# Gate and value products between the two row halves of the output products, three steps in front

## The chip, the core and the metric

The kernel runs on one core of one Trainium2 chip. The engines of the core are named as in the profile: PE (TensorE, matrix products), PEld (its weight loads), DVE (VectorE), ACT (ScalarE), POOL (GpSimd) and SP (SyncE, which here issues the transfers). The metric is the device time of one execution in microseconds (us), the median of the runs shown. A lower time is better.

## The reference

```python
scores = scale * np.matmul(x, state.transpose(0, 1, 3, 2))   # attention of x on the state, and back
...
x = np.ascontiguousarray(attn_out.transpose(0, 2, 1, 3)).reshape(B * S, H * D)   # 4352 rows x 512
x = _moe_ref(x=x, **moe_kwargs)          # soft mixture of 8 experts through 32 slots
...
g = x @ w_gate                           # 512 x 1536
silu = g * (1.0 / (1.0 + np.exp(-g)))
val = x @ w_val
return (silu * val @ w_out).astype(np.float32)
```

The last three lines are the part that the change touches. The rows of x are mixtures of 32 slots there, so the kernel multiplies the mixing weights (`cstack`) with folded gate and value weights (512 of x are folded to the slots once) instead of x with the full ones.

## The kernel before

**The main loop.** All rows are cut into 17 blocks of 256 rows (two tiles of 128), and the 1536 hidden columns into 6 pairs `q` of 2 x 128. One *step* is one block with one pair; there are 102. A function `plan()` puts the steps in order: first all blocks with pair 0, later longer runs of pairs (*segments*), so that the weights of a pair can be prepared while earlier pairs are used. The constants LEAD and RATE in it set when a new pair may come in. There are 51 segments.

A step has three parts, each a function, and their instructions go to the engines in program order; every engine works through its own queue in that order.

- `front(k)`: four products of 256 columns on PE (L1168), gates into one PSUM bank and values into another (`gvp`, two pairs of banks, taken in turn); then ACT's Silu (L1169) and DVE's product of value, scale and Silu (L1173), which writes `sh` (two buffers in turn).
- `middle(k)`: ACT's cast of that product to f16 (L1181) and POOL's difference to it (L1182): `hl`, a high and a low half.
- `back(k)`: twelve products of 512 columns on PE (L1204), six for each of the two row tiles i of the block, with `hl` as the stationary side and the output weights `WO` as the moving one. For each tile the first four products read the high half, the next two the low one. The two results stand in two of three accumulator banks `acc`, which are taken in turn: a segment's second bank is the one after the first. At a segment's last step both are evicted to `osb`, by ACT (L1231) in a block's first segment, and by DVE with an addition (L1233) in later ones.

In iteration k of the loop the order is `middle(k + 1)`, `front(k + 2)`, `back(k)`, the evictions of k, and then `spend`, which issues a bit of the background work. `hl` has two buffers, so the cast of k + 1 writes what `back(k - 1)` read.

**The background work** prepares the weights of the next pairs: POOL and DVE turn 64 bit words into f32 (`to32`: POOL L723, ACT L725, DVE L732 and L736), PE folds gates and values (L847), PE, DVE and ACT find their scales (L779 to L897), and ACT and DVE split the output weights (L812, L816). It is a generator with credits; each iteration takes 2 credits of it, or 1 where DVE has evictions to do. A fold comes one iteration or more after its last conversion was issued.

PSUM has eight banks: four for gates and values, three accumulators, one for the small products.

Of the kernel before, what the change touches and what calls it, by code (L numbers as in the profile page):

```python
# [8 lines left out]
F16 = mybir.dt.float16  # L9
# [3 lines left out]
AF = mybir.ActivationFunctionType  # L13
# [29 lines left out]
LEAD, RATE = 6, 21  # L43
# [41 lines left out]
def attn_moe_glu_kernel(  # L85
# [884 lines left out]
    def prep_first():  # L970
# [13 lines left out]
        for k in range(4):  # L984
            p2s.append((psum(k, [128, 512]) if k < 2 else gvp[1][k - 2])[:, 0:128])
            r = slice(32 * k, 32 * k + 32)
            pe.matmul(out=p2s[k], lhsT=Jrep[r, :], rhs=gt[r, :], start=True, stop=True)
# [67 lines left out]
    with tc.manual_schedule():  # L1055
# [90 lines left out]
        gvp = [[psum(3 + 2 * i + v, [128, 512]) for v in range(2)] for i in range(2)]  # L1146
# [8 lines left out]
        hls = [hlt[:, i] for i in range(2)]  # L1155

        def front(k, part=3):
            if k >= len(steps):
                return
            seg, bi, t0, q, _, _ = steps[k]  # L1160
            p, sh = gvp[k % 2], shs[k % 2]
            if part & 1:
                while 2 * q + 1 not in GV:
                    next(bg, None)
                rhs = cstack[:, t0:t0 + 2, :].rearrange("p t s -> p (t s)")
                for v in range(2):
                    for i in range(2):
                        pe.matmul(out=p[v][:, 256 * i:256 * i + 256], lhsT=GV[2 * q + i][v], rhs=rhs, start=True, stop=True)  # L1168
                act.activation(out=sh[:, 0, :], in_=p[0], func=AF.Silu, scale=sgs[q])  # L1169
            if part & 2:  # L1170
                while 2 * seg[1] - 1 not in GV:
                    next(bg, None)
                dve.scalar_tensor_tensor(out=sh[:, 1, :], in0=p[1], scalar=(kap0[0] if k == 0 else seg_scale(*seg)[0][q]), in1=sh[:, 0, :],  # L1173
                                         op0=ALU.mult, op1=ALU.mult)

        def middle(k):
# [3 lines left out]
            t = hls[k % 2]  # L1180
# [6 lines left out]
        def back(k):  # L1187
# [6 lines left out]
            accs = [acc[(2 * nblk[0] + i) % 3] for i in range(2)]  # L1194
            order = [(i, j, u) for i in range(2) for us in ((0, 1), (2,)) for j in range(2) for u in us]
            if k == 0:
                order.sort(key=lambda x: (x[1:] == (1, 1), x[2], x[1]))
            for i, j, u in order:
                while 2 * q + j not in WO:
                    next(bg, None)  # L1200
                c = slice(256 * j + 128 * i, 256 * j + 128 * i + 128)
                if i and k == len(steps) - 1:
                    continue
                pe.matmul(out=accs[i], lhsT=t[:, u // 2, c], rhs=WO[2 * q + j][:, u % 2, :],  # L1204
                          start=first and u == 0 and j == 0, stop=last and (j, u) == order[-1][1:])
            if k == len(steps) - 1:
                assert first
                for h in range(2):
                    hs = slice(256 * h, 256 * h + 256)
                    ph = (accs[1], psmall([128, 512]))[h]  # L1210
                    for n, (_, j, u) in enumerate(order[6:]):
                        c = slice(256 * j + 128, 256 * j + 256)
                        pe.matmul(out=ph[:, hs], lhsT=t[:, u // 2, c], rhs=WO[2 * q + j][:, u % 2, hs],  # L1213
                                  start=n == 0, stop=n == 5)
                    ends.append(ph)
            for i in range(2):
                a = accs[i]
                if not last:
                    continue
                o = osb[bi // 2][:, 2 * (bi % 2) + i, :]  # L1220
                rsc = segk[d, a_][1]
                if k == len(steps) - 1 and i:
                    r0 = ((t0 - 2) // 4) * ROWS + ((t0 - 2) % 4) * 128 + 128 * i
                    for h in range(2):
                        hs = slice(256 * h, 256 * h + 256)
                        dve.scalar_tensor_tensor(out=o[:, hs], in0=ends[h][:, hs], scalar=rsc, in1=o[:, hs],  # L1226
                                                 op0=ALU.mult, op1=ALU.add)
                        nc.sync.dma_start(out=out[r0:r0 + 128, hs], in_=o[:, hs])
                    continue
                if d == 0:  # L1230
                    act.activation(out=o, in_=a, func=AF.Copy, scale=rsc)  # L1231
                else:
                    dve.scalar_tensor_tensor(out=o, in0=a, scalar=rsc, in1=o, op0=ALU.mult, op1=ALU.add)  # L1233
                if k == len(steps) - 1:
                    r0 = ((t0 - 2) // 4) * ROWS + ((t0 - 2) % 4) * 128 + 128 * i
                    nc.sync.dma_start(out=out[r0:r0 + 128, :], in_=o)
# [10 lines left out]
            if t0:  # L1247
                r0 = ((t0 - 2) // 4) * ROWS + ((t0 - 2) % 4) * 128
# [21 lines left out]
        front(1, 2)  # L1270
        for k in range(len(steps)):
            middle(k + 1)
            front(k + 2)
            back(k)
            seg = steps[min(k + 4, len(steps) - 1)][0]
# [64 lines left out]
```

## Time and profile before

| | us |
|---|---|
| median of three runs | 470.25 (469.53 to 470.87) |
| the profiled execution | 469.4 |
| its span, first to last instruction | 467.6 |
| PE busy | 443.3 |
| DVE, ACT, POOL busy | 299.5, 251.1, 178.1 |
| span of the main loop's products, first L1204 start to its last | 138.4 to 462.5 |

A product that follows another is listed with its whole pass, so that rows overlap; the busy share of PE is therefore no measure of how many columns it took in. What matters is where PE stood idle, and what ended that.

### The profile page before, as it was taken

To read this page: it belongs to the slowest core of one execution; us is meant where nothing else is said; L and a number is where in the kernel's file an instruction comes from. 1 tells how busy PE (TensorE), PEld (TensorE's weight loads), DVE (VectorE), ACT (ScalarE), POOL (GpSimd) and SP (SyncE) were. 2 spreads that over 40 slices of the span, in tenths; PEclk is the share of its full clock that TensorE was granted. 3 is DMA by queue.
4 is the path that set the end of the run, shared out by engine and by line. 5 is a ranking of instruction groups with operands and counts; after the bars stand their busy time and mean duration, and the time that the engine had idled before them with its cause. 6 is when DMAs were issued, how large, how long until landed. Compare 5 with 4: busy or idle time off the path is not lost. (4 is left out here: it accounts for less than half of the span.)

```text
span 467.6 us, 9564 instructions
## 1 busy us (share of the span) xinstructions
PE 443.3 (95%) x3723; PEld 245.4 (52%) x3723; DVE 299.5 (64%) x629; ACT 251.1 (54%) x439; POOL 178.1 (38%) x160
## 2 busy tenths in 40 slices
PE   8799998999989999998998999999999999999997
PEld 6576765544454545444454454555555555555553
DVE  3777988467657888888998975544333433434555
ACT  2587877427348998764563535444444444444441
POOL 0113122073018656553573743433333333333331
PEclk9899999999999999999999999999999999999999
DMA  8999999799999407000000000000011111121224
GB/s 313 423 421 411 416 418 410 296 368 423 403 420 420 166 9 273 10 4 6 7 1 7 6 3 12 1 0 2 0 46 45 46 46 47 45 90 46 90 89 182
DMA packets 20060, 75.04 MB, mean 160 GB/s; under 512 B 5424, under 2 KB 7088, under 8 KB 13104
## 3 DMA queue, kind: packets, MB, share of 16 engines
q1 hardware_dynamic: 20016, 74.45, 40.1%
q8 instruction: 29, 0.48, 0.4%
q14 instruction: 15, 0.12, 0.1%
HBM read 64.87 MB, written 8.91 MB: 158 GB/s over the span
## 5 line engine op out<-in xcount | busy, mean ns | idle before, releaser
L1204 PE MATMUL p<-wo,hl 128*128 128x512 f16 x1014 | 233.9, 379 | 5.9 <-DVE osb L1233 3.0
L1182 POOL TENSOR_TENSOR hl<-sh,hl 128x512 f16<-128x512 f32 x102 | 123.4, 1210 | 198.3 <-PE p L1168 108.8
L1204 PEld LDWEIGHTS <-hl 128*128 128x128 f16 x1218 | 118.3, 98 | 131.3 <-POOL hl L1182 6.0
L1173 DVE SCALAR_TENSOR_TENSOR sh<-p,segk,sh 128x512 f32<-128x512 f32 x102 | 76.3, 748 | 102.5 <-ACT sh L1169 98.6
L1181 ACT CAST hl<-sh 128x512 f16<-128x512 f32 x102 | 62.9, 616 | 118.4 <-PE p L1204 90.4
L1169 ACT ACTIVATE sh<-p,sg 128x512 f32<-128x512 f32 x85 | 58.2, 685 | 5.6 <-PE p L1168 0.6
L1233 DVE SCALAR_TENSOR_TENSOR osb<-p,segm,osb 128x512 f32<-128x512 f32 x67 | 48.9, 745 | 11.6 <-PE p L1204 11.6
L1204 PE MATMUL p<-bqm,hl 128*128 128x512 f16 x204 | 47.0, 379 | 0.0
L1168 PE MATMUL p<-cstack,gvs 128*128 128x256 f16 x272 | 41.1, 273 | 0.6 <-DVE sh L1173 0.6
L357 POOL TENSOR_TENSOR a<-a,r 128x1024 f32<-128x1024 f32 x7 | 13.4, 1914 | 57.3 <-DVE r L353 16.3
L1168 PEld LDWEIGHTS <-gvs 128*128 128x128 f16 x272 | 25.8, 98 | 16.5 <-issue 1.8
L732 DVE SCALAR_TENSOR_TENSOR u<-u 128x512 uint32<-128x512 uint32 (+1 forms) x33 | 24.5, 753 | 5.1 <-POOL u L723 5.0
L723 POOL TENSOR_SCALAR u<-u 128x512 uint32<-128x512 uint8 x30 | 26.8, 892 | 2.5
L736 DVE SCALAR_TENSOR_TENSOR gvf<-gvf,u 128x512 uint32<-128x512 uint32 (+1 forms) x22 | 21.5, 994 | 0.2
L1168 PE MATMUL p<-cstack,gv 128*128 128x256 f16 x136 | 20.4, 273 | 0.0
L315 PE MATMUL p<-cs,atA 128*128 128x128 f32 x128 | 18.5, 285 | 1.7 <-DVE atA L280 0.5
L1231 ACT ACTIVATE osb<-p,segk 128x512 f32<-128x512 f32 x28 | 18.4, 693 | 2.7 <-PE p L1204 2.6
L310 ACT ACTIVATE atA<-atA,nm 128x512 f32<-128x512 f32 x16 | 10.7, 719 | 13.6 <-PE p L315 13.6
L1168 PEld LDWEIGHTS <-gv 128*128 128x128 f16 x136 | 13.2, 98 | 8.5
L315 PEld LDWEIGHTS p<-cs,atA 128*128 128x128 f32 x128 | 15.0, 146 | 3.6 <-DVE atA L280 1.0
L676 PE MATMUL p<-u,exq 128*32 128x256 f32 x256 | 15.2, 381 | 1.6 <-DMA u<-in_w_dram 0.8
L725 ACT ACTIVATE gvf<-u 128x512 f32<-128x512 f32 (+1 forms) x22 | 14.9, 723 | 0.0
(217 smaller groups left out, 452.9 us busy)
## 6 DMA issues: line engine op xcount, KB each, us to landing
u<-in_w_dram SPq DMA_DIRECT2D x24, 1024.0 KB, 14.5
u<-in_wgv_dram SPq DMA_DIRECT2D x12, 1024.0 KB, 17.4
u<-in_xn_dram SPq DMA_DIRECT2D x8, 1040.0 KB, 18.0
out_dram<-osb SPq DMA_DIRECT2D x15, 512.0 KB, 2.8
early<-in_w_dram SPq DMA_DIRECT2D x12, 512.0 KB, 10.4
u<-in_wo_dram SPq DMA_DIRECT2D x6, 1024.0 KB, 17.2
u<-in_xt_dram SPq DMA_DIRECT2D x3, 1024.0 KB, 7.1
early<-in_w_dram SPq DMA_DIRECT2D x1, 1024.0 KB, 8.9
```

Source lines behind the costliest of these rows:

```text
L315: pe.transpose(p[:, j, q * 128:(q + 1) * 128], stsA[:, q, j * 128:(j + 1) * 128], ident)
L723: pool.tensor_scalar(out=lo[:, c], in0=byte[:, c], scalar1=2.0 ** -5, scalar2=-31.0 / 64, op0=ALU.mult, op1=ALU.add)
L732: dve.scalar_tensor_tensor(out=lo[:, c], in0=hi[:, c], scalar=0x80000000, in1=lo[:, c], op0=ALU.bitwise_and, op1=ALU.bitwise_or)
L736: dve.scalar_tensor_tensor(out=tu[:, c], in0=tu[:, c], scalar=3, in1=lo[:, c], op0=ALU.logical_shift_left, op1=ALU.bitwise_or)
L1168: pe.matmul(out=p[v][:, 256 * i:256 * i + 256], lhsT=GV[2 * q + i][v], rhs=rhs, start=True, stop=True)
L1169: act.activation(out=sh[:, 0, :], in_=p[0], func=AF.Silu, scale=sgs[q])
L1173: dve.scalar_tensor_tensor(out=sh[:, 1, :], in0=p[1], scalar=(kap0[0] if k == 0 else seg_scale(*seg)[0][q]), in1=sh[:, 0, :], op0=ALU.mult ...
L1181: act.copy(out=t[:, 0, :], in_=sh[:, 1, :])
L1182: pool.tensor_tensor(out=t[:, 1, :], in0=sh[:, 1, :], in1=t[:, 0, :], op=ALU.subtract)
L1204: pe.matmul(out=accs[i], lhsT=t[:, u // 2, c], rhs=WO[2 * q + j][:, u % 2, :], start=first and u == 0 and j == 0, stop=last and (j, u) == ...
L1231: act.activation(out=o, in_=a, func=AF.Copy, scale=rsc)
L1233: dve.scalar_tensor_tensor(out=o, in0=a, scalar=rsc, in1=o, op0=ALU.mult, op1=ALU.add)
```

## The change

The iteration becomes: first half of `back(k)` (tile 0) and its eviction, `front(k + 3)`, `middle(k + 2)`, second half of `back(k)` (tile 1) and its eviction, background work. `back` is now a generator that is left and entered again between its halves (not at step 0, where all twelve products come first). The buffers of `hl` become three; the third lies where an early tile of the kernel (`sp`) had been. Before the loop, `middle(1)` and `front(2)` are issued as well. The bank pairs and the three accumulators are the same banks as before, written in another form. LEAD goes from 6 to 7, which moves the joints between segments from step 24 on (there are 51 segments as before), and `seg_scale` looks one step further ahead.

```diff
@@ -40,7 +40,7 @@
 H2 = 0
 H7 = 0
 HP_ = 0, 1
-LEAD, RATE = 6, 21
+LEAD, RATE = 7, 21
 CR = 1.0
 CN = 2.0
 YM = 5
@@ -982,7 +982,7 @@
         gv = [gvs[:, 0, v] for v in range(2)]
         p2s = []
         for k in range(4):
-            p2s.append((psum(k, [128, 512]) if k < 2 else gvp[1][k - 2])[:, 0:128])
+            p2s.append((psum(k, [128, 512]) if k < 2 else gvp[k])[:, 0:128])
             r = slice(32 * k, 32 * k + 32)
             pe.matmul(out=p2s[k], lhsT=Jrep[r, :], rhs=gt[r, :], start=True, stop=True)
         mw = sm.tile([128, 1], F32, tag="mw1", bufs=1, name="mw")
@@ -1143,7 +1143,7 @@
         expert_o(1)
         ps1.close()
         ps.append(ctx.enter_context(tc.tile_pool(name="ps2", bufs=1, space=PSUM)))
-        gvp = [[psum(3 + 2 * i + v, [128, 512]) for v in range(2)] for i in range(2)]
+        gvp = [psum(3 + i, [128, 512]) for i in range(4)]
         steps = []
         for bi, d, a in plan():
             for q in range(d, a):
@@ -1152,13 +1152,13 @@
         osb = {}
         shs = [wk.tile([128, 2, 512], F32, tag=f"a{i}", name="sh") for i in range(2)]
         hlt = wk.tile([128, 2, 2, 512], F16, tag="e2", name="hl")
-        hls = [hlt[:, i] for i in range(2)]
+        hls = [hlt[:, i] for i in range(2)] + [wk.tile([128, 2, 512], F16, tag="sp", name="hl")]
 
         def front(k, part=3):
             if k >= len(steps):
                 return
             seg, bi, t0, q, _, _ = steps[k]
-            p, sh = gvp[k % 2], shs[k % 2]
+            p, sh = [gvp[(2 * k + v) % 4] for v in range(2)], shs[k % 2]
             if part & 1:
                 while 2 * q + 1 not in GV:
                     next(bg, None)
@@ -1177,7 +1177,7 @@
             if k >= len(steps):
                 return
             sh = shs[k % 2]
-            t = hls[k % 2]
+            t = hls[k % 3]
             act.copy(out=t[:, 0, :], in_=sh[:, 1, :])
             pool.tensor_tensor(out=t[:, 1, :], in0=sh[:, 1, :], in1=t[:, 0, :], op=ALU.subtract)
             hl[k] = t
@@ -1192,48 +1192,48 @@
                 room[0] -= 1
                 room[1] -= 1
             accs = [acc[(2 * nblk[0] + i) % 3] for i in range(2)]
+            end = k == len(steps) - 1
             order = [(i, j, u) for i in range(2) for us in ((0, 1), (2,)) for j in range(2) for u in us]
             if k == 0:
                 order.sort(key=lambda x: (x[1:] == (1, 1), x[2], x[1]))
-            for i, j, u in order:
-                while 2 * q + j not in WO:
-                    next(bg, None)
-                c = slice(256 * j + 128 * i, 256 * j + 128 * i + 128)
-                if i and k == len(steps) - 1:
-                    continue
-                pe.matmul(out=accs[i], lhsT=t[:, u // 2, c], rhs=WO[2 * q + j][:, u % 2, :],
-                          start=first and u == 0 and j == 0, stop=last and (j, u) == order[-1][1:])
-            if k == len(steps) - 1:
-                assert first
-                for h in range(2):
-                    hs = slice(256 * h, 256 * h + 256)
-                    ph = (accs[1], psmall([128, 512]))[h]
-                    for n, (_, j, u) in enumerate(order[6:]):
-                        c = slice(256 * j + 128, 256 * j + 256)
-                        pe.matmul(out=ph[:, hs], lhsT=t[:, u // 2, c], rhs=WO[2 * q + j][:, u % 2, hs],
-                                  start=n == 0, stop=n == 5)
-                    ends.append(ph)
-            for i in range(2):
-                a = accs[i]
-                if not last:
-                    continue
-                o = osb[bi // 2][:, 2 * (bi % 2) + i, :]
-                rsc = segk[d, a_][1]
-                if k == len(steps) - 1 and i:
-                    r0 = ((t0 - 2) // 4) * ROWS + ((t0 - 2) % 4) * 128 + 128 * i
+            parts = [order, []] if k == 0 else [order[0:6], order[6:12]]
+            r0 = ((t0 - 2) // 4) * ROWS + ((t0 - 2) % 4) * 128
+            for part in range(2):
+                i = part
+                if end and i:
+                    assert first and last
                     for h in range(2):
                         hs = slice(256 * h, 256 * h + 256)
-                        dve.scalar_tensor_tensor(out=o[:, hs], in0=ends[h][:, hs], scalar=rsc, in1=o[:, hs],
-                                                 op0=ALU.mult, op1=ALU.add)
-                        nc.sync.dma_start(out=out[r0:r0 + 128, hs], in_=o[:, hs])
-                    continue
-                if d == 0:
-                    act.activation(out=o, in_=a, func=AF.Copy, scale=rsc)
+                        ph = (accs[1], psmall([128, 512]))[h]
+                        for n, (_, j, u) in enumerate(parts[1]):
+                            c = slice(256 * j + 128, 256 * j + 256)
+                            pe.matmul(out=ph[:, hs], lhsT=t[:, u // 2, c], rhs=WO[2 * q + j][:, u % 2, hs],
+                                      start=n == 0, stop=n == 5)
+                        ends.append(ph)
                 else:
-                    dve.scalar_tensor_tensor(out=o, in0=a, scalar=rsc, in1=o, op0=ALU.mult, op1=ALU.add)
-                if k == len(steps) - 1:
-                    r0 = ((t0 - 2) // 4) * ROWS + ((t0 - 2) % 4) * 128 + 128 * i
-                    nc.sync.dma_start(out=out[r0:r0 + 128, :], in_=o)
+                    for x, j, u in parts[part]:
+                        while 2 * q + j not in WO:
+                            next(bg, None)
+                        c = slice(256 * j + 128 * x, 256 * j + 128 * x + 128)
+                        pe.matmul(out=accs[x], lhsT=t[:, u // 2, c], rhs=WO[2 * q + j][:, u % 2, :],
+                                  start=first and u == 0 and j == 0, stop=last and (j, u) == order[-1][1:])
+                if last:
+                    o = osb[bi // 2][:, 2 * (bi % 2) + i, :]
+                    rsc = segk[d, a_][1]
+                    if end and i:
+                        for h in range(2):
+                            hs = slice(256 * h, 256 * h + 256)
+                            dve.scalar_tensor_tensor(out=o[:, hs], in0=ends[h][:, hs], scalar=rsc, in1=o[:, hs],
+                                                     op0=ALU.mult, op1=ALU.add)
+                            nc.sync.dma_start(out=out[r0 + 128:r0 + 256, hs], in_=o[:, hs])
+                    elif d == 0:
+                        act.activation(out=o, in_=accs[i], func=AF.Copy, scale=rsc)
+                    else:
+                        dve.scalar_tensor_tensor(out=o, in0=accs[i], scalar=rsc, in1=o, op0=ALU.mult, op1=ALU.add)
+                    if end and not i:
+                        nc.sync.dma_start(out=out[r0:r0 + 128, :], in_=o)
+                if not part:
+                    yield
             if k == len(steps) - 1:
                 assert t0
                 return
@@ -1245,7 +1245,6 @@
             ob = osb[bi // 2]
             c = 2 * (bi % 2)
             if t0:
-                r0 = ((t0 - 2) // 4) * ROWS + ((t0 - 2) % 4) * 128
                 nc.sync.dma_start(out=out[r0:r0 + 256, :].rearrange("(i p) d -> p i d", p=128), in_=ob[:, c:c + 2, :])
             else:
                 for b in range(B):
@@ -1268,11 +1267,15 @@
         acc = [psum(i, [128, 512]) for i in range(3)]
         middle(0)
         front(1, 2)
+        middle(1)
+        front(2)
         for k in range(len(steps)):
-            middle(k + 1)
-            front(k + 2)
-            back(k)
-            seg = steps[min(k + 4, len(steps) - 1)][0]
+            half = back(k)
+            next(half)
+            front(k + 3)
+            middle(k + 2)
+            run(half)
+            seg = steps[min(k + 5, len(steps) - 1)][0]
             if k and all(2 * q + 1 in GV for q in range(*seg)):
                 seg_scale(*seg)
             spend(bg, CR if steps[k][5] and steps[k][0][0] else CN)
```

Three places show how instructions move on an engine. POOL, at the start of the main loop (`hl` is written by L1182 of `middle`, `u` by L723, the first part of a conversion; the L622 rows belong to the stage before the loop):

```order
 L622 TENSOR_TENSOR cc_1658<-cc,cc_1658 128x2x32 x2
-L1182 TENSOR_TENSOR hl<-sh,hl 128x512 x2
+L1182 TENSOR_TENSOR hl<-sh,hl 128x512 x3
 L723 TENSOR_SCALAR u<-u 128x512 x2
 L1182 TENSOR_TENSOR hl<-sh,hl 128x512
```

The first conversion stood behind the low halves of steps 0 and 1, and stands behind those of 0, 1 and 2 now.

ACT, in iterations 21 to 23 before (`two_2864` is the scaled fold of pair 3, which needs DVE's scales; `hl` the cast, `sh` the Silu, `wo16` the output weights):

```order
L1181 CAST hl_1978<-sh_1976 128x512
L1169 ACTIVATE sh_1977<-p5_1974,sg_2335 128x512
L890 ACTIVATE two_2864<-bqm_1980,sc_2856 128x128
L1181 CAST hl_1978<-sh_1977 128x512
L1169 ACTIVATE sh_1976<-p3_1972,sg_2335 128x512
L1181 CAST hl_1978<-sh_1976 128x512
L1169 ACTIVATE sh_1977<-p5_1974,sg_2601 128x512
L812 ACTIVATE wo16_2930<-wof_2728,sc_2856 128x512 x2
```

and the same place after the change:

```order
L1169 ACTIVATE sh_1976<-p3_1972,sg_2344 128x512
L1181 CAST hl_1979<-sh_1977 128x512
L890 ACTIVATE two_2873<-bqm_1981,sc_2865 128x128
L1169 ACTIVATE sh_1977<-p5_1974,sg_2344 128x512
L1181 CAST hl_1978<-sh_1976 128x512
L1169 ACTIVATE sh_1976<-p3_1972,sg_2610 128x512
L1181 CAST hl_1978<-sh_1977 128x512
L812 ACTIVATE wo16_2939<-wof_2737,sc_2865 128x512 x2
```

The cast that stood right behind L890 was that of step 23, which PE takes in the next iteration; it is that of step 24 now, and step 23's cast stands ahead of L890. Within an iteration the Silu comes before the cast.

DVE, where the weights of pair 4 are split (L816), before (`osb` by L1233 are the two evictions of one block; `sh` is L1173):

```order
L897 SCALAR_TENSOR_TENSOR two_3174<-bqm_1980,sc_3167,two_3174 128x128
L816 SCALAR_TENSOR_TENSOR wo16_3222<-wof_3048,sc_3167,wo16_3222 128x512 x2
L1173 SCALAR_TENSOR_TENSOR sh_1977<-p6_1975,segk_2816,sh_1977 128x512
L1233 SCALAR_TENSOR_TENSOR osb_2373<-p2_2066,segm_2815,osb_2373 128x512
L1233 SCALAR_TENSOR_TENSOR osb_2373<-p0_2064,segm_2815,osb_2373 128x512
L736 SCALAR_TENSOR_TENSOR gvf_3105<-gvf_3105,u_2419 128x512
```

and after (the eviction has the line number 1232 there):

```order
L897 SCALAR_TENSOR_TENSOR two_3187<-bqm_1981,sc_3180,two_3187 128x128
L1232 SCALAR_TENSOR_TENSOR osb_2374<-p2_2067,segm_2824,osb_2374 128x512
L1173 SCALAR_TENSOR_TENSOR sh_1977<-p6_1975,segk_3142,sh_1977 128x512
L1232 SCALAR_TENSOR_TENSOR osb_2374<-p0_2065,segm_2824,osb_2374 128x512
L816 SCALAR_TENSOR_TENSOR wo16_3231<-wof_3057,sc_3180,wo16_3231 128x512 x2
L1173 SCALAR_TENSOR_TENSOR sh_1976<-p4_1973,segk_3142,sh_1976 128x512
```

The first eviction of a block stands ahead of the product L1173 of the iteration and the second behind it, and here both stand ahead of the split that was ahead of them.

## Rows read from the trace of the kernel before

**Rows 1.** The page's costliest groups: busy us, mean ns of one | idle before.

```profile
L1204 PE MATMUL p<-wo,hl 128*128 128x512 f16 x1014 | 233.9, 379 | 5.9 <-DVE osb L1233 3.0
```

**Rows 2.** PE's waits over the whole program: in total us, times, longest.

```profile
PE p L1204 <- DVE osb L1233: 3.0, 4, 1.5
PE p L1204 <- POOL hl L1182: 1.9, 5, 0.9
...
PE p L1204 <- ACT hl L1181: 1.0, 2, 0.8
...
PE s L847 <- DVE gvf L736: 0.9, 2, 0.4
...
PE s L785 <- DVE D L783: 0.3, 1, 0.3
```

**Rows 3.** Timeline of one undisturbed step: start us, us, engine, line; idle before.

```profile
301.21 0.62 ACT L1181 CAST hl<-sh 128x512 f16<-128x512 f32 x1 [1.63 <-PE p L1204]
...
301.45 0.60 PE L1168 MATMUL p<-cstack,gv 128*128 128x256 f16 x4
...
301.88 2.75 PE L1204 MATMUL p<-wo,hl 128*128 128x512 f16 x12
301.91 1.15 POOL L1182 TENSOR_TENSOR hl<-sh,hl 128x512 f16<-128x512 f32 x1 [1.87 <-PE p L1168]
301.93 0.69 ACT L1169 ACTIVATE sh<-p,sg 128x512 f32<-128x512 f32 x1
302.70 0.75 DVE L1173 SCALAR_TENSOR_TENSOR sh<-p,segk,sh 128x512 f32<-128x512 f32 x1 [2.27 <-ACT sh L1169]
...
304.91 2.75 PE L1204 MATMUL p<-bqm,hl 128*128 128x512 f16 x12
```

**Rows 4.** Timeline, iterations 0 to 4, with the first fold.

```profile
140.84 1.92 POOL L723 TENSOR_SCALAR u<-u 128x512 uint32<-128x512 uint8 x2
141.02 1.26 ACT L1231 ACTIVATE osb<-p,segk 128x512 f32<-128x512 f32 x2 [0.90 <-PE p L1204]
...
141.47 2.75 PE L1204 MATMUL p<-wo,hl 128*128 128x512 f16 x12
...
145.27 2.41 POOL L723 TENSOR_SCALAR u<-u 128x512 uint32<-128x512 uint8 x2
...
148.99 2.57 DVE L736 SCALAR_TENSOR_TENSOR gvf<-gvf,u 128x512 uint32<-128x512 uint32 x2
...
149.48 1.90 PE L1204 MATMUL p<-wo,hl 128*128 128x512 f16 x8 [0.94 <-POOL hl L1182]
...
151.31 1.08 PE L847 MATMUL s<-gvf,ST 128*32 128x128 f32 x32
...
152.77 2.75 PE L1204 MATMUL p<-wo,hl 128*128 128x512 f16 x12
```

**Rows 5.** Timeline, iterations 22 and 23.

```profile
217.28 0.40 ACT L890 ACTIVATE two<-bqm,sc 128x128 f16<-128x128 f32 x1 [5.09 <-DVE sc L888]
217.59 0.60 ACT L1181 CAST hl<-sh 128x512 f16<-128x512 f32 x1
...
218.25 1.04 PE L1204 MATMUL p<-wo,hl 128*128 128x512 f16 x4 [0.75 <-ACT hl L1181]
```

**Rows 6.** Timeline, iterations 34 to 36.

```profile
255.61 0.74 DVE L1173 SCALAR_TENSOR_TENSOR sh<-p,segk,sh 128x512 f32<-128x512 f32 x1
256.27 1.39 DVE L1233 SCALAR_TENSOR_TENSOR osb<-p,segm,osb 128x512 f32<-128x512 f32 x2
...
257.06 1.46 PE L1204 MATMUL p<-wo,hl 128*128 128x512 f16 x6 [1.47 <-DVE osb L1233]
...
264.28 1.46 PE L1204 MATMUL p<-wo,hl 128*128 128x512 f16 x6 [1.00 <-DVE osb L1233]
```

**Rows 7.** Lines L736 and L1182 on their own: duration ns min/median/max.

```profile
L736 DVE SCALAR_TENSOR_TENSOR gvf<-gvf,u x22: 671/684/1668, 107.8 to 264.8; 128x512 uint32<-128x512 uint32 x20, 128x1024 uint32<-128x1024 uint32 x2
L1182 POOL TENSOR_TENSOR hl<-sh,hl x102: 1152/1157/3000, 138.5 to 459.3; 128x512 f16<-128x512 f32 x102
```

## The prediction

> **What bounds the kernel now.** I read the page first, then PE's waits, then the timeline of one step, then the timeline at each place where PE waits. The page's costliest group is the output product L1204 [rows 1]. In an undisturbed step, twelve of them are listed with 2.75 us, and the next twelve start 3.03 us after the first [rows 3]. With 0.379 us listed for one [rows 1], the pitch is (2.75 - 0.379) / 11 = 0.216 us; four products of the front take the remaining 3.03 - 12 x 0.216 = 0.44. So PE is full there: nothing but its own columns bounds a step, and the change takes none of them away. The 102 steps are 309 us.
>
> What it can win is the idle time in the loop, and the reader is to see in PE's waits how little that is [rows 2]: L1204 waits 3.0 us for accumulators (DVE L1233), 1.9 for the low half (POOL), 1.0 for the high half (ACT), and there are 0.9 for folds and 0.3 for a scale. A wait in this view begins when the listed 0.379 ends, not when the next product could have started, so each is 0.379 - 0.216 = 0.16 longer. With that: accumulators 3.0 + 4 x 0.16 = 3.6; POOL 1.9 + 5 x 0.16 = 2.7; ACT's large one 0.75 + 0.16 = 0.9 [rows 5]; the scale 0.4; folds 1.2. ACT's other one comes at step 0, where the change alters nothing.
>
> **The change, part by part.**
>
> *The order in ACT's and POOL's queues.* Background work of iteration k stands directly ahead of the cast and the difference for step k + 2 before, and ahead of those for k + 3 after; PE asks for those 3.03 us later. On ACT a Silu (0.69) has come between, so the delay that is borne grows by 2.3 us there and by 3.0 on POOL. The waits of this kind are 0.9 [rows 5] and at most 1.1 (0.94 + 0.16) [rows 4]. The casts themselves are no earlier: before, the difference ends 301.91 + 1.15 - 301.88 = 1.2 us after the step's start, and PE reads it at its next step's fifth product, 3.03 + 0.86; spare 2.7. After, the front begins at 6 x 0.216 = 1.3, Silu 0.48 later (301.93 - 301.45), cast and difference behind it end at about 4.2, and are read at 6.06 + 0.86; spare 2.7 again. The third `hl` buffer takes away the cast's wait for PE, 1.63 us [rows 3], which cost PE nothing. I take both sums as gone: 2.7 + 0.9 = **3.6** (bounds: 1.5, if POOL's small waits come back elsewhere, and 3.6). With the queue relieved the scale's 0.4 goes as well (bounds 0 and 0.4).
>
> *The accumulators.* Before, the evictions of a block stand behind L1173 on DVE, which is late: L1173 at 255.61, then both evictions, then PE [rows 6]. After, the first stands ahead of it: 0.66 us (256.27 - 255.61). Its bank is asked for again six products, a front and six products later before (12 x 0.216 = 2.6, and 0.44), and with another front after: 0.44 more. Together 1.1 us of each wait; the two large ones are 1.47 + 0.16 and 1.00 + 0.16 [rows 6]. The second bank is asked for as long after the first as before. LEAD moves the evictions of this stretch to other steps, and the split L816 now stands behind them. I take all **3.6** (bounds: 2.2 from the 1.1 twice, and 3.6).
>
> *Folds: the cost.* DVE's background work of iteration k stands behind L1173 of step k + 3, not k + 2. Where ACT evicts, nothing else stands ahead of it: it starts at 1.3 + 1.25 + 0.75 = 3.3 us of the step after, and at 302.70 + 0.75 - 301.88 = 1.6 before; 1.7 later. The fold on PE is only one front (0.44) later, so 1.3 us of spare are lost at each of the first three folds. Later, where DVE evicts, the work is behind the second eviction both times and nothing is lost in the order itself.
>
> The first fold is the worst place, since POOL's queue there begins late. Before, POOL's first conversion starts at 140.84 [rows 4]. After, it is behind the difference of step 2, which is behind ACT's first eviction (141.02), Silu and cast (about 0.6 each, 142.8) and its own 1.16: 144.0. The second conversion was at 145.27, and its L736 ended at 148.99 + 2.57 = 151.56, which is 6.3 later. After, it is behind the difference of step 3, whose cast comes after an eviction, two L725, an eviction and a Silu on ACT (about 0.6 each: 146.1), so that the difference ends at about 147.4 to 148.0; plus 6.3 is 153.7 to 154.3. The second half of the fold (0.5) needs it, and the step behind starts at 154.4 to 155.0 against 152.77 before. PE without a wait would reach the fold at 141.47 + 3 x 3.03 = 150.6 and that step at 151.7, so the wait is about **3.0** us where there was none; the wait of 1.1 ahead of it, counted as gone above, is given back, and more. Bounds: 1.8, if the two L736 take 0.68 each and not 2.57 together, and 4.0, if one more of DVE's two-input passes meets POOL (1.67 against 0.68) [rows 7]. Second and third fold: 1.3 for both together beyond what they wait for now (bounds 0 and 2.6; the middle, as part of ACT's lateness there goes too). Fourth and fifth: 0.5 (bounds 0 and 2), since DVE is behind there and loses its pauses.
>
> What the durations hang on here is that L736 takes from 0.67 to 1.67 us and the difference from 1.15 to 3.0 [rows 7]; the long ones lie beside each other. The Trainium skill, "SBUF — State Buffer", "Who interferes with whom", says why: a VectorE instruction with two SBUF inputs and a GpSimd one that reads SBUF exclude each other, and the one that comes second stands still until the first has ended. The trace agrees. By that rule a change that moves POOL's differences onto DVE's conversions would lose up to 1.16 us at each meeting; the 4.0 above would become 4.2.
>
> *Edits at nothing.* The halves cost PE no switch, as there are as many changes between front and back as before (the next product starts 0.43 us after a front's first, 301.88 - 301.45). `middle(1)` and `front(2)` ahead of the loop are issued in the same order on each engine. The third buffer lies where nothing is in use. At the end the last step's first eviction is the only thing that moves, and PE's last products set the end.
>
> **The sum.** 3.6 + 0.4 + 3.6 = 7.6 won, 3.0 + 1.3 + 0.5 = 4.8 lost: 2.8 us. On the profiled execution's own 469.4 this gives 466.6. That execution is 0.85 below the median of the runs shown, 470.25, from which it gives 467.45. I say **467.0**, between both.
>
> **Rivals.**
>
> *Nothing left over.* DVE is behind from iteration 20 to 36, and PE's waits are only how the delay shows. Then the accumulators keep 3.6 - 2.2 = 1.4, fourth and fifth fold cost 2, and 7.6 - 1.4 - (3.0 + 1.3 + 2) = -0.1 is left: 469.5 to 470.35. For it: DVE's row at 256.27 follows L1173 without a pause. Against: the first eviction is 1.1 us better off.
>
> *Slower: the folds.* Every fold waits as the first does, because conversion and fold are still an iteration apart while the conversion's engines run behind later steps. Five times 3.0 less the 1.2 of now is 13.8 lost, 6.2 more than won: 475.6 to 476.5. It turns slower (by more than 0.3%, or 1.4 us, which is about what a measurement of this kernel can tell from no change) once the folds wait (7.6 + 1.2 + 1.4) / 5 = 2.0 us on average. For it: the first one, worked out above, and the two L736 of 2.57 us. Against: the later ones have no start in which POOL's queue is shifted by a whole step, and for the last two the order on DVE is no worse.
>
> *All won.* The first fold waits only 1.8 and the others no longer than now: 7.6 - 1.8 = 5.8, so 463.6 to 464.5. For it: at the first fold PE's wait lets all other engines get ahead, so that later ones meet finished work.
>
> **Chances.** Forecast 0.47 (465 to 468.6), nothing left 0.25, folds 0.12, all won 0.16. The range from 463.4 to 470.9 leaves out most of the slow rival and little else. Faster by over 0.3% (under 468.8): the forecast nearly whole and all won, 0.62. Within 0.3%: 0.25. Slower: 0.13.
>
> **What the profile after would show.** PE's waits for `hl` from ACT and POOL behind step 0 gone, and the one for L1233 at or near nothing. Instead a wait of L847 for L736, of 2 to 4 us, near 151, with the step behind it at about 154.7. The step at 3.03 us in the second half of the loop, and ACT's cast there following the Silu without a wait for PE. The prediction is wrong if the step is longer than 3.03, if PE waits for a gate bank (L1168 for L1173), or if the folds after the first wait over 1.5 us each.

## The result, and the profile after

| | before | after |
|---|---|---|
| median us (6 runs each) | 469.51 (468.11 to 470.87) | 474.80 (473.54 to 478.39) |
| profiled execution, its span | 469.4, 467.6 | 473.88, 472.1 |
| first to last start of the output products in the loop | 138.4 to 462.5 | 139.0 to 467.0 |

The changed kernel is slower: 1.012 of the time before, 95% interval 1.0079 to 1.0161. The span grew by 4.5 us: 0.6 ahead of the loop (its start lies between 136.8 and 139.6 in the kernels measured here, none of which changes anything there) and 3.9 in it.

PE's waits in the loop of the changed kernel (140 to 462 us; in total us, times, longest) answer to [rows 2]:

```profile
PE s L847 <- DVE gvf L736: 6.8, 4, 2.5
PE s L785 <- DVE D L783: 1.8, 1, 1.8
PE p L1218 <- DVE osb L1232: 1.2, 1, 1.2
```

All waits for `hl` are gone, and the accumulators' are down from four to one. But the folds (L847) went from 0.9 to 6.8 and a scale (L785) from 0.3 to 1.8. With the prediction's 0.16 added to each, PE's idle time in the loop is 9.8 + 6 x 0.16 = 10.8 now. Before it was 6.9 + 13 x 0.16 = 9.0 (in the same stretch; ACT's first wait of [rows 2] lies ahead of it). That is 1.8 of the 3.9.

The rest is the clock. The page's row of granted clock, 40 slices of 11.8 us, falls in the second slice, long before the loop, and once more within it:

```profile
PEclk9799999999999999998999999999999999999999
```

The windows around that place (us; then busy time and instructions of PE, PEld, DVE, ACT, POOL; granted clock, DMA share, GB/s):

```profile
139.00:221.50 82.50, 73.82 (x459) 37.85 (x460) 67.64 (x128) 62.00 (x109) 51.54 (x44) 1.00 0.35 138
221.50:225.00 3.50, 3.50 (x12) 1.55 (x11) 3.36 (x12) 0.36 (x2) 0.00 (x0) 0.51 0.01 2
225.00:460.00 235.00, 233.76 (x1288) 121.18 (x1287) 129.50 (x227) 102.11 (x174) 99.15 (x86) 1.00 0.09 32
```

For 3.5 us PE runs at 0.51, the lower of its two levels (1.2 GHz), and does half the work: 1.7 us lost. The row before it in the timeline is the long wait for the scale, which ends at 220.89. So 1.8 + 1.7 = 3.5 of the 3.9 are accounted for. Before, the loop had no such slice.

The timeline shows the three folds that wait, and the scale (after; [rows 4] are the first fold before):

```profile
144.69 1.91 POOL L723 TENSOR_SCALAR u<-u 128x512 uint32<-128x512 uint8 x2
...
148.42 2.25 POOL L723 TENSOR_SCALAR u<-u 128x512 uint32<-128x512 uint8 x2
...
150.07 2.71 DVE L732 SCALAR_TENSOR_TENSOR u<-u 128x512 uint32<-128x512 uint32 x2
...
151.22 0.41 PE L847 MATMUL s<-gvf,ST 128*32 128x128 f32 x4
...
152.71 0.74 DVE L1173 SCALAR_TENSOR_TENSOR sh<-p,segk,sh 128x512 f32<-128x512 f32 x1
153.37 1.28 DVE L736 SCALAR_TENSOR_TENSOR gvf<-gvf,u 128x512 uint32<-128x512 uint32 x2
...
154.10 1.23 PE L847 MATMUL s<-gvf,ST 128*32 128x128 f32 x28 [2.47 <-DVE gvf L736]
...
155.26 1.04 PE L1218 MATMUL p<-wo,hl 128*128 128x512 f16 x4
...
172.66 2.75 PE L1218 MATMUL p<-wo,hl 128*128 128x512 f16 x12
...
173.56 2.59 DVE L816 SCALAR_TENSOR_TENSOR wo<-wof,sc,wo 128x512 f16<-128x512 f32 x2
...
176.07 0.68 DVE L732 SCALAR_TENSOR_TENSOR u<-u 128x512 uint32<-128x512 uint32 x1
...
177.08 0.41 PE L847 MATMUL s<-gvf,ST 128*32 128x128 f32 x4
...
178.44 1.28 DVE L736 SCALAR_TENSOR_TENSOR gvf<-gvf,u 128x512 uint32<-128x512 uint32 x2
...
179.17 1.23 PE L847 MATMUL s<-gvf,ST 128*32 128x128 f32 x28 [1.67 <-DVE gvf L736]
...
205.05 0.64 PE L847 MATMUL s<-gvf,ST 128*32 128x128 f32 x16 [2.24 <-DVE gvf L736]
...
206.11 0.63 PE L847 MATMUL s<-gvf,ST 128*32 128x128 f32 x12 [0.42 <-DVE gvf L736]
...
215.87 1.46 PE L1218 MATMUL p<-wo,hl 128*128 128x512 f16 x6
...
217.51 0.74 DVE L1173 SCALAR_TENSOR_TENSOR sh<-p,segk,sh 128x512 f32<-128x512 f32 x1
...
220.62 0.22 DVE L783 TENSOR_SCALAR D<-cs,D 3x3 f32<-3x3 f32 x1
...
220.89 0.38 PE L785 MATMUL s<-D,cs 3*128 3x3 f32 x2 [1.79 <-DVE D L783]
```

PE's first four fold products (151.22) need only the first of the fold's two converted tiles, which is long finished; the next 28 wait until DVE (L736) has written the second tile, and DVE has stood behind L1173 of a later step. The second fold shows where DVE's chain hangs, and before is the measure:

```profile
168.43 2.75 PE L1204 MATMUL p<-wo,hl 128*128 128x512 f16 x12
...
169.24 1.84 DVE L816 SCALAR_TENSOR_TENSOR wo<-wof,sc,wo 128x512 f16<-128x512 f32 x2
...
172.76 1.90 PE L1204 MATMUL p<-wo,hl 128*128 128x512 f16 x8 [0.28 <-POOL hl L1182]
...
173.25 2.26 DVE L736 SCALAR_TENSOR_TENSOR gvf<-gvf,u 128x512 uint32<-128x512 uint32 x2
...
174.59 1.60 PE L847 MATMUL s<-gvf,ST 128*32 128x128 f32 x32
...
210.12 0.75 DVE L1173 SCALAR_TENSOR_TENSOR sh<-p,segk,sh 128x512 f32<-128x512 f32 x1 [1.08 <-ACT sh L1169]
...
210.54 2.75 PE L1204 MATMUL p<-wo,hl 128*128 128x512 f16 x12
...
213.27 0.22 DVE L783 TENSOR_SCALAR D<-cs,D 3x3 f32<-3x3 f32 x1
...
213.54 0.38 PE L785 MATMUL s<-D,cs 3*128 3x3 f32 x2 [0.25 <-DVE D L783]
```

From the start of L816 to the end of the second L736 it is 173.25 + 2.26 - 169.24 = 6.3 us before, and 178.44 + 1.28 - 173.56 = 6.2 after: the chain is no longer. But it starts 0.8 us after the step's first output product before (168.43), and 2.6 after it in the changed kernel: the first half of that step's products lies six products and a front (1.30 + 0.43) ahead of the row at 172.66, which starts with its second half, so the step starts at 172.66 - 1.73 = 170.93. The conversion is 1.8 us later in the step (1.7 in the prediction). PE comes to the fold no later at all: 174.59 - 168.43 = 6.2 us after the step's first product before, and 177.08 - 170.93 = 6.2 after. The front that now stands ahead of the fold takes up the time of the wait for `hl` that is gone (0.28 + 0.16).

The scale (L785) is the same case. From the start of L1173 to the end of L783 it is 3.4 us before (210.12 to 213.49) and 3.3 after (217.51 to 220.84), but this chain starts 0.4 us ahead of the step's first output product before (210.54) and 1.6 behind it after (215.87).

### The profile page after: what moved, and what is told of

It is laid out like the page before. It is cut to its first block, busy times and chain, and to the rows that moved or that the text cites. A ratio compares the mean times of both kernels' runs of the same rounds, so it can differ in the third digit from the quotient of the medians.

```text
span 472.1 us, 9485 instructions
## 1 busy us (share of the span) xinstructions
PE 445.3 (94%) x3723; PEld 248.4 (53%) x3723; DVE 304.0 (64%) x625; ACT 245.6 (52%) x439; POOL 180.9 (38%) x160
## 4 chain that ended last, share of the span: by engine, by line
PE 74%; DVE 11%; DMA 5%; ACT 5%; issue 4%; POOL 1%; SPq 0%; DVEq 0%; ACTq 0%; POOLq 0%
PE p L1218 49%; PE p L1168 8%; DMA u<-in_w_dram 4%; PE p L315 3%; PE p L270 2%; PE s L370 2%; PE p L645 1%; DVE u L732 1%; PE p L250 1%; DMA u<-in_xt_dram 1%; DVE gvf L736 1%; DVE sh L1173 1%; PE s L847 1%; ACT sh L1169 1%; PE p L391 1%
## 5 line engine op out<-in xcount | busy, mean ns | idle before, releaser
L1218 PE MATMUL p<-wo,hl 128*128 128x512 f16 x1014 | 238.1, 381 | 1.5 <-DVE osb L1232 1.2
L1182 POOL TENSOR_TENSOR hl<-sh,hl 128x512 f16<-128x512 f32 x102 | 124.2, 1218 | 196.8 <-ACT hl L1181 196.3
L1173 DVE SCALAR_TENSOR_TENSOR sh<-p,segk,sh 128x512 f32<-128x512 f32 x102 | 76.3, 748 | 85.0 <-ACT sh L1169 82.8
L1232 DVE SCALAR_TENSOR_TENSOR osb<-p,segm,osb 128x512 f32<-128x512 f32 x67 | 50.1, 747 | 22.9 <-PE p L1218 22.7
L1218 PE MATMUL p<-bqm,hl 128*128 128x512 f16 x204 | 49.6, 379 | 0.0
L732 DVE SCALAR_TENSOR_TENSOR u<-u 128x512 uint32<-128x512 uint32 (+1 forms) x33 | 26.8, 820 | 13.4 <-POOL u L723 13.2
L723 POOL TENSOR_SCALAR u<-u 128x512 uint32<-128x512 uint8 x30 | 28.8, 959 | 2.5
L736 DVE SCALAR_TENSOR_TENSOR gvf<-gvf,u 128x512 uint32<-128x512 uint32 (+1 forms) x22 | 19.8, 925 | 0.2
```

The lines of the kernel that those rows point to most:

```text
L723: pool.tensor_scalar(out=lo[:, c], in0=byte[:, c], scalar1=2.0 ** -5, scalar2=-31.0 / 64, op0=ALU.mult, op1=ALU.add)
L732: dve.scalar_tensor_tensor(out=lo[:, c], in0=hi[:, c], scalar=0x80000000, in1=lo[:, c], op0=ALU.bitwise_and, op1=ALU.bitwise_or)
L736: dve.scalar_tensor_tensor(out=tu[:, c], in0=tu[:, c], scalar=3, in1=lo[:, c], op0=ALU.logical_shift_left, op1=ALU.bitwise_or)
L1182: pool.tensor_tensor(out=t[:, 1, :], in0=sh[:, 1, :], in1=t[:, 0, :], op=ALU.subtract)
L1218: pe.matmul(out=accs[x], lhsT=t[:, u // 2, c], rhs=WO[2 * q + j][:, u % 2, :], start=first and u == 0 and j == 0, stop=last and (j, u) == ...
L1232: dve.scalar_tensor_tensor(out=o, in0=accs[i], scalar=rsc, in1=o, op0=ALU.mult, op1=ALU.add)
```

## The experiments

Theory A, the order: DVE's and POOL's background work stands behind a product and a difference of one more step, the fold on PE has kept its place, and PE waits there. Its rival B: DVE and POOL hold each other up more, or DVE has too much to do, so that the time is lost wherever the fold stands. LEAD, the third buffer and the clock were tried too. Ratios are against runs of the kernel before on the same chip; "loop" is from the first to the last start of an output product in the profiled execution.

| | median us | ratio (95%) | loop us |
|---|---|---|---|
| changed, once more (e5) | 475.87 | 1.0138 (1.0118 to 1.0157) | 330.7 |
| changed, fold a step later (e1) | 467.66 | 0.9968 (0.9942 to 0.9993) | 323.3 |
| changed, whole back (e2) | 471.92 | 1.0037 (1.0019 to 1.0056) | 325.4 |
| before, third buffer (e3) | 470.94 | 1.0023 (1.0003 to 1.0044) | 324.9 |
| changed, background ahead of the front (e4) | 469.63 | 1.0017 (0.9994 to 1.0040) | 324.9 |
| changed, LEAD 6 (e6) | 477.03 | 1.0174 (1.0141 to 1.0206) | 333.8 |
| before, fold later (e7) | 466.07 | 0.9933 (0.9919 to 0.9947) | 321.4 |
| changed, fold later, spread (e8) | 466.19 | 0.9936 (0.9918 to 0.9953) | 321.0 |
| changed, filled folds (e9) | 473.45 | 1.0099 (1.0075 to 1.0122) | 328.2 |
| before, fold later, spread (e10) | 464.70 | 0.9912 (0.9892 to 0.9932) | 319.2 |
| changed, both later, spread (e11) | 462.74 | 0.9870 (0.9847 to 0.9893) | 317.8 |
| before, both later, spread (e12) | 464.27 | 0.9902 (0.9874 to 0.9931) | 318.7 |

**The fold one place later (e1).** In the preparation of a pair, just ahead of the fold, the generator gives way once more:

```diff
         yield "S"
+        yield "S"
         p = psmall([128, 128])
```

> The changed kernel, with each fold (L847) one iteration later in the background work, nothing else. Theory A (the conversions stand behind the product and the difference of three steps ahead, so they are late at folds that come at the same place as before): the waits of L847 for L736, 7.4 us in the changed kernel, fall under 1.5, and the time comes to 464 to 468 us. Rival B (DVE and POOL simply have more to do, because their passes meet more often): the 7 us come back as waits for scales, accumulators or hl, and the time stays at 472 to 475.

PE's waits in its loop:

```profile
PE p L1219 <- DVE osb L1233: 2.8, 2, 1.5
PE s L779 <- DVE mx L872: 2.0, 2, 1.2
PE s L847 <- DVE gvf L736: 1.5, 1, 1.5
PE p L1169 <- DVE sh L1174: 0.4, 1, 0.4
PE p L1169 <- DMA gvs<-two: 0.3, 1, 0.3
```

Of 6.8 us at the folds 1.5 are left, and the whole is 7 us shorter by the ratios, from 1.2% slower to 0.3% faster. That is what theory A expected. Part of B holds too: 3.6 us have come up at other places where PE meets DVE (2.0 at L779, and 1.6 more at accumulators).

**The halves undone (e2), and the background work moved ahead of the front (e4).**

```diff
-            half = back(k)
-            next(half)
             front(k + 3)
             middle(k + 2)
-            run(half)
+            run(back(k))
```

> The changed kernel with front(k + 3) and middle(k + 2) ahead of a whole back(k), instead of between its halves: three steps of lead and three buffers stay. Theory A, in the form that the half step (1.3 us) of later start is what the folds lose: the waits of L847 fall to about 1.5 to 3 us, those for hl stay gone, and the time comes to 467 to 470. If it is the lead of three steps that puts POOL's differences ahead of the conversions, not the half: the first fold still waits 2 to 3 us, and the time is 470 to 473. Rival B: 472 to 475.

Three steps in front and three buffers, but PE does all twelve products before the fold and behind the front. The fold waits are 2.8 us in three: by fold 1.0, none and 1.8, where they were 2.5, 1.7 and 2.7. That is 1.3 shorter in the mean, the half step (6 x 0.216), though single folds gained from 0.9 to 1.7. The accumulator waits are back with 3.5 in four: both sides of the split in one kernel. The time, 471.92, lies above the 467 to 470 of theory A, with these waits beside it; the sign of the other branch, a first fold that still waits 2 to 3 us, is not there. In e4 `seg_scale` and `spend` stand right behind the first half, ahead of `front(k + 3)`, so that DVE's conversions precede L1173 of step k + 3:

> The changed kernel with the background work of iteration k (seg_scale and spend) right after the first half of back(k), ahead of front(k + 3) and middle(k + 2). Conversions then stand ahead of the product and the difference of that iteration, and the fold 1.73 us earlier on PE. Theory A: the waits of L847 together 1 to 4 us (before: 1.2), the time 467 to 471. Rival B: 472 to 475.

The folds wait 2.3 us in three, the low half 0.5 and the high half not at all; 2.2 us at L779 are new. The time is that of before within the measurement: 4.5 of the 6.8 us at the folds go when the conversions stand ahead in DVE's queue, and half of that comes back at L779.

**The buffer alone (e3) and LEAD alone (e6).** In e3 the kernel before has the third `hl` buffer (`hls[k % 3]`) and nothing else:

> The kernel before with three buffers of hl and nothing else. The cast no longer waits for PE (90 us of waits in total, none of them PE's). Theory A: ACT gets ahead, the order in the queues is the old one, and folds wait as before; the waits for hl (3.6 us) fall by half; 466.5 to 469.5. If the buffer alone brings POOL's differences onto DVE's conversions (rival B): folds wait more and the time is 470 to 473.

Its waits are those of before (accumulators 2.9, POOL 2.1, ACT 1.2), so the expectation that the waits for `hl` fall by half missed: they come from the queues, not from the buffer. Its time, 470.94, is in the range of the rival, but the folds wait 0.9 us as before, so the rival's sign is missing too. In e6 only `LEAD, RATE = 6, 21` is put back in the changed kernel:

> The changed kernel with LEAD back at 6: the joints between segments as before. It changes nothing ahead of step 24, where three folds and the scale wait lie. If the order in the queues is the cause: 472 to 475, as the changed kernel. If the moved joints cost something: 2 us or more below the changed kernel.

The folds wait 7.0 us, the accumulators 2.1, L779 1.3 and L785 1.2, and at 477.03, above all that was expected, it is no faster than the changed kernel: LEAD 7 isn't the cause.

**The changed kernel once more (e5), and its folds filled (e9).**

> The changed kernel as it is, beside the others on one chip, for its granted clock over more runs (the profile had 3.4 us at half clock at 221.6, behind PE's wait of 1.95 us for a scale, and a mean of 0.988 against 0.995). If the lower clock belongs to the change (long idle stretches of PE bring it), the median clock of these runs is 0.988 to 0.993 where the kernel before has 0.996, and the time 473 to 475. If it was chance, the clock is 0.995 to 0.996 and the time 471 to 472.5.

The time (475.87) and the median clock (0.9875) went a little beyond the range for a clock that belongs to the change. PE's waits agree to 0.1 us with those of the first profile, yet the loop is 2.7 longer. Its long waits, and its windows (columns as above), say why:

```profile
152.75 1.92 PE L847 MATMUL s<-gvf,ST 128*32 128x128 f32 x28 [2.45 <-DVE gvf L736]
...
204.83 0.64 PE L847 MATMUL s<-gvf,ST 128*32 128x128 f32 x16 [2.26 <-DVE gvf L736]
...
222.34 0.38 PE L785 MATMUL s<-D,cs 3*128 3x3 f32 x2 [1.79 <-DVE D L783]
```

```profile
152.20:155.70 3.50, 2.95 (x31) 1.79 (x32) 2.38 (x4) 2.18 (x5) 2.65 (x3) 0.51 1.01 417
155.70:206.80 51.10, 46.73 (x294) 23.95 (x293) 43.50 (x90) 39.88 (x72) 31.14 (x27) 1.00 0.20 75
206.80:210.30 3.50, 3.50 (x12) 1.51 (x10) 1.71 (x4) 2.12 (x5) 0.00 (x0) 0.51 0.00 0
210.30:223.90 13.60, 11.81 (x62) 5.96 (x61) 11.67 (x23) 6.19 (x11) 6.95 (x6) 1.00 0.01 2
223.90:227.30 3.40, 3.40 (x12) 1.51 (x10) 2.82 (x12) 1.22 (x3) 0.00 (x0) 0.50 0.00 0
```

There are three such stretches here, and each begins at a long wait of PE or within 1.6 us behind it: the first fold (2.45 us), the third (2.26 and 0.42) and the scale (1.79). Three times 1.7 and 1.8 of waits are 6.9; the loop is 6.6 longer than before. In e6 there are three as well, at the three folds (waits of 2.48, 1.62, and 2.43 with 0.43):

```profile
155.30:158.70 3.40, 3.40 (x22) 1.45 (x19) 1.74 (x3) 1.48 (x4) 2.81 (x3) 0.51 0.76 318
182.60:186.00 3.40, 3.40 (x11) 1.46 (x10) 1.81 (x3) 2.13 (x5) 2.09 (x3) 0.51 0.42 104
209.90:213.40 3.50, 3.50 (x19) 1.50 (x20) 2.49 (x4) 1.40 (x3) 0.46 (x1) 0.52 0.02 5
```

But not every such wait is followed by one. Of eleven of 1.6 us or more at folds and scales in the first profile, e5 and e6, seven are (one, three and three); in the first profile all three folds (2.47, 1.67, 2.24 with 0.42) are not.

To test whether the waits bring the lower clock, e9 puts eight products of 512 columns ahead of each of the first three folds; their result is read by nobody:

```diff
         yield "S"
+        hz = psmall([128, 512])
+        if q < 4:
+            for _ in range(8):
+                pe.matmul(out=hz, lhsT=cstack[:, 0, :], rhs=cstack[:, 0:4, :].rearrange("p t s -> p (t s)"), start=True,
+                          stop=True)
```

> The changed kernel with eight products of 512 columns (f16, result unused, 1.7 us) on PE ahead of each of the first three folds, where PE waits 1.8 to 3.0 us anyway; they add work and leave none out. If PE's idle stretch is what brings the half clock of 3.4 us behind it (seen behind the first and third fold and the scale wait in two profiles), the granted clock rises from 0.989 to about 0.993 to 0.996, the waits of L847 shrink by the time of the filling, the loop's waits and filling together stay as they are, and the time falls by 1.7 to 3.5 us, to 471 to 473.5. If the clock falls for another reason, it stays at 0.986 to 0.990 and the time at 474 to 477.

It adds 3 x 1.7 us to PE's work and is faster than e5, by 2.4 us of the medians on the same chip (1.0099 to 1.0138 in ratios, 1.8 us, with intervals that just touch). Its windows:

```profile
139.00:158.00 19.00, 18.30 (x120) 9.28 (x119) 12.55 (x16) 15.86 (x29) 13.13 (x12) 1.00 0.87 362
158.00:206.00 48.00, 47.02 (x294) 23.82 (x291) 41.93 (x88) 37.38 (x66) 30.74 (x26) 1.00 0.20 72
206.00:222.00 16.00, 14.21 (x77) 7.30 (x76) 13.90 (x27) 8.55 (x15) 6.94 (x6) 1.00 0.01 2
222.00:460.00 238.00, 235.21 (x1295) 121.62 (x1294) 133.33 (x238) 102.90 (x175) 99.72 (x86) 1.00 0.09 31
```

No stretch of the loop is at the lower level. The folds wait 1.5 us, so that waits and filling together are what the waits were. The loop is 2.5 us shorter than that of e5 with its three stretches, and as long as that of the first profile with one (328.0), as the accumulators now wait 2.8 us and not 1.2. The mean clock of this execution is 0.989 all the same: it ran at the lower level ahead of the loop, mostly from 130.3 to 137.9 us (0.55 there), where PE's listed waits are 0.4 us at most. Over the six executions the median is 0.994 against e5's 0.9875. So the filling goes with a higher clock, but long waits are neither always followed by the lower level nor the only thing ahead of it. The wait for the scale is there as before, 1.79 us, and this time nothing follows it: why a wait does it in one execution and not in another stays open.

**What the old order does with the same late fold (e7), and with the work spread (e8, e10).** e7 is the edit of e1 in the kernel before:

> The kernel before with each fold one iteration later. If what the later fold wins is the lateness that the three-step order brings, there is little to win here (folds wait 1.2 us): 468 to 470. If DVE is simply short of time around the folds whatever the order, PE's waits for hl move and the time falls as much as in the changed kernel: 463 to 466.

It came out below the 468 to 470 expected if there was little to win, and next to the 463 to 466 of the other branch. So part of the conversions were late in the old order too; PE's waits there are now 3.2 for accumulators and 1.8 for POOL's `hl`. The old order wins 0.7% by the later fold (3.2 us), the changed one 1.5% to 1.7%: what the changed order had lost against the old one, 1.2% to 1.4%, shrinks to 0.35% (0.9968 to 0.9933, each against the kernel before on its own chip). That much of the loss hangs on the place of the fold; the rest of what e1 won, the old order can win too. e8 is e1, e10 is e7, both with fewer credits per iteration and an earlier start (`CN = 1.8`, `LEAD, RATE = 9, 22`), which thins the background work:

> The changed kernel with each fold one iteration later, and the background work spread over more iterations: 1.8 credits an iteration and not 2, LEAD 9 and RATE 22 so that no pair is asked for early (58 segments, 14 evictions more on DVE, most where it has time). If DVE's backlog between iterations 5 and 40 is what still waits in the kernel with the later fold (accumulators 2.8, the reduction ahead of the scales 2.0, a fold 1.5): 464 to 466.5. If the order within the iteration alone is the cause, no change: 467 to 468.

> The kernel before with each fold one iteration later and the background work spread as in the kernel of the changed order that was spread (1.8 credits, LEAD 9, RATE 22). If order and spread win independently, 463 to 465; if the later fold had already taken what there is in the old order, 465.5 to 467, and the three-step order wins nothing over the old one with the same background work.

In e8 the scale waits 2.3 us, the accumulators 2.3; in e10 the accumulators 2.4 and POOL's `hl` 1.2. With these edits alone the old order is 1.5 us better, and the scale (L785), at which the old order doesn't wait, is the largest part of the changed order's own loss that is left.

**Both late (e11, e12).** The fold as in e1, and one more place for the scale; `CN = 1.9`, `LEAD, RATE = 11, 22`. e12 is the same in the order of before:

```diff
         yield "S"
+        yield "S"
         pe.matmul(out=p[:, 128:128 + n], lhsT=vb[:n].to_broadcast([n, 128]), rhs=D[:, 0:n], start=True, stop=True)
```

> The changed kernel with the fold and also the second product of the scales (L785) one iteration later each, 1.9 credits, LEAD 11 and RATE 22 (58 to 60 segments). PE's waits for scales (2.3 us in the spread kernel) go: 463 to 465.5. If DVE's lateness only moves on to the accumulators: 465.5 to 467.5.

> The same three edits on the kernel before. It tells whether the three-step order is worth anything once nothing waits for folds and scales: if it is, this one is 1 us or more slower than the changed order with the same edits; if not, equal or faster.

PE's waits in the loop of e11:

```profile
PE p L1220 <- DVE osb L1234: 1.1, 2, 0.7
PE s L779 <- DVE mx L873: 1.1, 2, 0.9
PE p L1170 <- DVE sh L1175: 0.4, 1, 0.4
```

Nothing waits for a fold or a scale any more, and nothing for `hl`. At 0.987 (6.3 us) it is faster than both kernels, and a little below what was expected. In the order of before the same edits give 0.990, with 1.9 us left for accumulators and 0.9 for `hl`: so the change itself may be worth 0.9 us (loop) to 1.5 us (medians) once the meeting places have moved with it, but the intervals overlap, and this gain is not shown beyond the noise. CN and LEAD were set anew together with the place of the scale, so what each of them brings was not told apart.

## Why the prediction was wrong

- **Right: the waits for `hl`.** All 3.6 us went, and the step kept its 3.03 us.
- **Nearly right: the accumulators.** One wait of 1.2 + 0.16 is left of the 3.6, so 2.2 were won, its lower bound. With LEAD 6 (e6) 2.1 + 3 x 0.16 = 2.6 are left, so part of this gain goes with the moved joints.
- **Right: the first fold.** Conversions at 144.69 and 148.42 (144.0 and about 148 foretold), the step behind at 155.26 (154.4 to 155.0), and the wait 2.47 + 0.16 = 2.6 us (3.0). The long pass stands elsewhere than foretold, in L732 (2.71 us) and not in L736 (1.28); from the second conversion to the end of L736 it is 6.2 us, near the 6.3 that the prediction carried over.
- **Wrong: "Second and third fold: 1.3 for both together".** This is the step that failed most. With the 0.16 they wait 1.8 and 3.0 us, against none listed and 1.2 before: 3.6 more. Both are over the 1.5 that the prediction itself named as a sign of being wrong. The prediction worked out the right delay (1.7 later on DVE, 0.44 on PE, 1.3 of spare lost) and then set it against spare that wasn't there. DVE's chain to the second fold (6.3 us) had none before: it ended at 175.51, inside the row of fold products that starts at 174.59 and takes 1.60 us, where the first fold takes 1.08. It also expected that with ACT's and POOL's lateness gone some of the delay would go. But PE's wait for `hl` stood *ahead* of the fold, and DVE's chain runs beside it; PE without that wait makes up for the front and comes to the fold as early as before, and waits there instead. At these three folds, what was won at `hl` was given back.
- **Wrong: "the scale's 0.4 goes as well".** It grew to 1.95, 1.6 more: L785 is a meeting of the same kind, and DVE's part of it starts 2.0 us later against PE's step, of which the front covers 0.44.
- **Right: the fourth and fifth fold.** They don't wait; so "Every fold waits as the first does" was right of three of five, and the rival's 2.0 us per fold was not reached (7.4 / 5 = 1.5). That the time came near this rival's 475.6 to 476.5 is in part luck: the scale and the clock, which it doesn't have, stand in for two folds that don't wait.
- **Missing: the clock.** The prediction has no term for it. PE's waits moved little in sum, 1.8 us. But few long ones stand where many short ones were, and behind some of the long ones PE ran at the lower level for 3.4 us at a time, once to three times in the loop of the profiled executions. Less 1.7 us for each, the loop would be 1.5 to 2.2 us longer than before, and not 3.9 and 6.6.

By its own terms: 3.6 + 2.2 won, 1.6 lost at the scale, 6.2 at folds, 1.7 to the clock, is 3.7 us slower; 3.9 were measured.

That the larger part of the loss is the order of the queues against the place of the fold is shown by e1 beside e7 (with the later fold in both, the changed order is 0.35% behind and not 1.2% to 1.4%), and borne out by e4 (the conversions moved ahead) and e2 (half a step given back). That DVE and POOL hold each other up more isn't needed for the folds: at the third the pair of L736 takes 2.70 us after and 2.72 before. The Trainium skill's rule of "SBUF — State Buffer", "Who interferes with whom", explains why such a pair is longer than two L736 on their own (0.67 us each [rows 7]), but not why it came to matter. How much of e1's new waits at L779 is collision and how much is total load was not told apart.

## What to carry to other kernels

When work is issued further in front, list for each engine what then stands behind it, and for each of those the fixed place where another engine waits for it; move these places by as much. A wait that is removed ahead of such a meeting reappears there if the meeting is bound by a third engine. Compare waits by length, not only by sum.

## What the runs showed of the hardware

In a loop that is otherwise full, PE's granted clock fell to half for about 3.4 us behind seven of eleven waits of 1.6 to 2.5 us at folds and scales (first profile, e5, e6), which costs up to 1.7 us, nearly as much as the wait itself; what sets the seven apart from the other four the runs do not show. Eight unused products (1.7 us) in front of each of the first three folds left no such stretch in the loop of the profiled execution (e9), and that kernel, with more work, was 1.8 us faster by the ratios, at the edge of what the intervals tell.
